# Attention and two expert layers in one kernel: first value sums and second query sums on GpSimd, the token list zeroed from a ready tile, the last gate logits ahead of the first expert job, and gate logits with the token tile as weights

## The chip, the cores and the metric

The kernel runs on one core of one Trainium2 chip. The time is device microseconds (us) for one execution. Three runs of the kernel before gave a median of 747.64 us (745.11 to 751.28). The engines are called by the names of the profile: PE is TensorE, DVE is VectorE, ACT is ScalarE, POOL is GpSimd, SP is SyncE, which issues most DMAs.

## What is computed

Attention over 4 batches, 8 heads, 576 tokens and a head width of 64, in two parts that are added; then two mixture-of-experts layers on the 2304 tokens of width 512. Each has 8 experts with a hidden width of 1024 and sends a token to one expert.

```python
q_d, k_d, v_d = (mean over groups of 4 tokens of q, k, v)
out_up    = repeat(softmax(q_d k_d^T * scale) v_d, 4)
out_local = softmax(q k^T * scale, only |i - j| < 4) v
x = out_up + out_local                       # 2304 x 512

logits = x @ w_gate;  e = argmax(logits);  g = softmax(logits)[e]
layer 1: out = g * sigmoid(x @ w_output_gate)[e] * (relu(x @ w1[e]) @ w2[e])
layer 2: the same on the result, without the sigmoid
```

## The kernel before

**Attention.** The tokens are cut into 20 tiles of 2 x 58 tokens (5 tiles a batch). For each batch the sums of 4 neighbours are formed of k (`sums_k`, L442), q (`sums_q`, L459) and v (`sums_v`, L478). From them come "pooled" scores, a softmax, and `od`, which is spread over the tiles by a matmul with `rep`. Each tile adds its local attention (class `Local`, L593). `sums_v` adds, for each of three blocks, two halves of `vraw` (L480, 128x520) and then twice 64x260 into `vpd` (L483): 3 and 6 instructions a batch. On POOL, `sums_k` and `sums_q` take two steps through a tile `tm` (L451 and L457; L475 and L476); on DVE, `sums_q` is one reduction (L473).

**The order of the work.** A prologue is written out by the string `PRO` (L72): `F` first sums, `V0` the value sums of batch 0 on DVE, `s`, `m`, `f` the pooled attention of its four head pairs, `A0` and `A2` the sums of batch 1 (the engines given by `S1` at L71: of the four letters, k and q of each half, "p" is POOL and "d" DVE), `V1` the value sums of batch 1 on POOL, `list` the opening of the token list. Then steps -1 to 22 follow, each by the string `ORDER` (L73): the pooled work of the next batch, the scores of tile s, the values of tile s-1, the transposes and logits of tile s-2, and routing. A scheduler orders the instructions of each engine from that; each engine then runs its list strictly in order and waits on semaphores.

**The token list.** `list_open` (L239) starts an accumulation of zeros in PSUM: it makes a zero tile by multiplying a constant with 0 and three copies on DVE, and one matmul (L247). Each tile then adds its tokens with one matmul (`put`, L357), made from `am`, `oc` and `bm` (L344 to L353).

**Gate logits of a tile** (L696 to L712): four matmuls with the gate columns (32) as weights and the token tile as the moving side (L377 in `logits`), a copy to SBUF on ACT (L702), and one matmul with the copied 128x128 block as weights and a selection of 16 columns (L709); then a copy on DVE (L712) into `lgs`. `route` (L251) picks the expert of each token, counts with `tri` and `ones` (L286 to L293, result `pos`), computes the place in the list (`place`, L307) and spreads it.

**Experts.** The first job (256 tokens of the largest expert, chosen by `snap` after 14 tiles) gathers its rows by indirect DMA on POOL (`fetch`, L1161; `gather`, L1149), transposes them (`xpose`, L1192; PE L1201, ACT L1205 for `xh`, DVE L1208 for `xl`) and runs `hide` (L1397): per 128 hidden units 12 matmuls (L1283 to L1285) with the weights split into `wh` and `wl` (L1122 on ACT, L1130 on DVE), then the second layer into `py`. The raw weights come through three buffers (`raw`). The second job needs the list of all 20 tiles. Behind the first job stands a loop over overflow slots (L1291), at which all engines meet; behind it come the other jobs of both layers, which fill the time from 206 us to the end.

Of the kernel before, what the change touches and what calls it, by code (L numbers as in the profile page):

```python
# [9 lines left out]
F32 = mybir.dt.float32  # L10
# [4 lines left out]
ALU = mybir.AluOpType  # L15
# [17 lines left out]
LK = E * NS  # L33
# [26 lines left out]
LGX = 1  # L60
# [7 lines left out]
QPE = 2  # L68
KPOOL = 0
Q1POOL = 0  # L70
S1 = "pdpd"  # L71
PRO = "F0 s0 V0 s1 F2 s2 s3 zq m1 Ls m0 m2 f0 f1 lqk lvr f2 m3 V1 A0 lcs rep A2 f3 Le lvw zp lw1 list"  # L72
ORDER = "R As Ae q0f Cf Xt Cp p0s Xl Xs An p0e q1f p1s q0p Cx D p1e K q1p S"  # L73

C_ID = 0
# [105 lines left out]
def moe_pair_kernel(  # L181
# [17 lines left out]
    nc = tc.nc  # L199
# [5 lines left out]
    ps_misc = ctx.enter_context(tc.tile_pool(name="ps_misc", bufs=1, space=PSUM))  # L205
# [10 lines left out]
    wgs = [const.tile([128, 4, 32], F32, name=f"wg{i}") for i in range(2)]  # L216
# [4 lines left out]
    ikey = cs[:, C_IKEY:C_IKEY + LK]  # L221
    sel = cs[:, C_SEL:C_SEL + 16]
# [12 lines left out]

    list_ps = {}
    placed = {}

    def list_open(m):  # L239
        t = ps_list.tile([128, 512], F32, tag="list", name=f"list{m}")  # L240
        z = ab.tile([128, 3 * LK], F32R, tag="bm", name="zb")
        za = ab.tile([128, 128], F32R, tag="am", name="za")
        nc.vector.tensor_scalar(z[:, 0:LK], ikey, 0.0, None, op0=ALU.mult)
        nc.vector.tensor_copy(z[:, LK:2 * LK], z[:, 0:LK].bitcast(F32))
        nc.vector.tensor_copy(z[:, 2 * LK:3 * LK], z[:, 0:LK].bitcast(F32))
        nc.vector.tensor_copy(za, z[:, 0:128].bitcast(F32))
        nc.tensor.matmul(t[:, 0:3 * LK], lhsT=za, rhs=z, start=True, stop=False, skip_group_check=True)  # L247
        nc.vector.memset(base[m], 0.0)
        list_ps[m] = t
# [125 lines left out]
    def logits(m, xT, n, lT, after=None):  # L375
        for g in range(4):
            i = nc.tensor.matmul(  # L377
                lT[32 * g:32 * g + 32, 0:n], lhsT=wgs[m][:, g, :], rhs=xT[:, g, 0:n],
                tile_position=(0, 32 * g), start=True, stop=True, skip_group_check=True,
            )  # L380
            if after is not None:
                tc.add_manual_dep(
                    i.ins, after.ins.name,
                    mybir.DependencyInfo(mybir.DependencyClass.Sync, mybir.DependencyReason.DATA),
                    reason="the four column tiles run side by side",
                )


    def attention(actx, early, early_x, front):
# [3 lines left out]
        sb2 = actx.enter_context(tc.tile_pool(name="a_sb2", bufs=2, side="right"))  # L393
# [11 lines left out]
        rep = sb1.tile([128, NTP + NP, 128], F32R, name="rep")  # L405
# [3 lines left out]
        zx = sbe.tile([128, DM], F32, name="zx")  # L409
# [68 lines left out]
        def sums_v(b, eng=nc.gpsimd):  # L478
            for k in range(3):
                eng.tensor_tensor(vraw[:, k, 0:2], vraw[:, k, 0:2], vraw[:, k, 2:4], op=ALU.add)  # L480
                for s in range(2):
                    o = slice(64 * s, 64 * s + 64)
                    eng.tensor_tensor(vpd[b % 2][o, k, s], vraw[o, k, 0], vraw[o, k, 1], op=ALU.add)  # L483
# [109 lines left out]
        class Local:  # L593
# [100 lines left out]
                front[0] = nc.scalar.copy(self.xT, self.pt)  # L694

            def lmm(self):  # L696
                self.lT = ps_misc.tile([128, 4, 128], F32, tag="misc", name="lT")
                logits(0, self.xT, 128, self.lT[:, 0])

            def ltevac(self):  # L700
                self.lts = sb2.tile([128, 128], F32, tag="lts", name="lts")
                nc.scalar.copy(self.lts, self.lT[:, 0])  # L702

            def lsel(self):
                if LGX:
                    self.lg = self.lT[:, 1, 0:16]
                else:
                    self.lg = ps_misc.tile([128, 512], F32, tag="misc", name="lg")[:, 0:16]
                nc.tensor.matmul(self.lg, lhsT=self.lts, rhs=sel, skip_group_check=True)  # L709

            def lgevac(self, lgs, j):
                nc.vector.tensor_copy(lgs[:, j], self.lg)  # L712
# [4 lines left out]
        for b in range(B):  # L717
            s0 = NTP * (b - 1) + 2
# [19 lines left out]
        wu = ps_misc.tile([128, 512], F32, tag="misc", name="wu")  # L738
        for _ in range(NWARM):
            nc.tensor.matmul(wu, lhsT=zx[:, 0:128], rhs=zx)  # L740
        load_k(0, 0, 2)
        load_q(0, 0, 2)
        nc.sync.dma_start(ident, cst[:, C_ID:C_ID + 128])
# [39 lines left out]
        def sums1(c):  # L783
            sums_k(1, c, 2, None if S1[c] == "d" else nc.gpsimd)
            sums_q(1, c, 2, None if S1[c + 1] == "d" else nc.gpsimd)

        pro = {
            "F0": lambda: first(0),
            "F2": lambda: first(2),
            "V0": lambda: sums_v(0, nc.vector),  # L790
            "Ls": lambda: (loc[0].scores(), loc[0].smax()),
            "Le": loc[0].exps,
            "rep": staged,
            "list": lambda: list_open(0),
            "zp": lambda: zero(1, nc.gpsimd, "p"),
            "zq": lambda: zero(1, nc.gpsimd, "q"),
            "lvw": lambda: load_vw(0),
# [8 lines left out]
        for c in range(NP):  # L806
            pro.update({
                f"s{c}": lambda c=c: start(c), f"m{c}": lambda c=c: middle(c), f"f{c}": lambda c=c: finish(c),
            })
        for o in PRO.split():  # L810
            pro[o]()

        for s in range(-1, NL + 3):
# [4 lines left out]
            A, C, X = get(s), get(s - 1), get(s - 2)  # L818
# [61 lines left out]
                    ]  # L880

            def xsel():
                X.lsel()
                if g[1] == 0:
                    lgst[g[0]] = sb2.tile([128, 5, 16], F32, tag="lgs", name="lgs")
                X.lgevac(lgst[g[0]], g[1])
# [11 lines left out]
                "Cx": C and C.xevac,  # L898
                "Ct": C and (lambda: (C.xflip(), C.xtevac())),
                "Xt": X and (lambda: (X.xflip(), X.xtevac())),  # L900
                "Xl": X and (lambda: (X.lmm(), X.ltevac())),
                "Xs": X and xsel,
                "K": group, "D": defer1, "R": ready1, "S": puts1,
            }
# [60 lines left out]
    def experts():  # L965
# [226 lines left out]
        def xpose(job, k):  # L1192
            if k == 0:
                xp = pl[f"x{job.i % 2}"]
                job.xT = tuple(xp.tile([128, 4, 512], F32R, tag=t, name=t) for t in ("xh", "xl"))
            xh, xl = job.xT
            mm = job.slots[k][1]
            xr = job.x[k]
            pt = psx.tile([128, 4, 128], F32, tag="m", name="t")
            for d in range(4):  # L1200
                nc.tensor.transpose(  # L1201
                    pt[:, d, 0:mm], xr[0:mm, 128 * d:128 * d + 128], ident[0:mm, 0:mm]
                )
            o = slice(128 * k, 128 * k + mm)
            i = nc.scalar.copy(xh[:, :, o], pt[:, :, 0:mm])  # L1205
            if job.i == 0:
                after.append(i)
            nc.vector.tensor_tensor(xl[:, :, o], pt[:, :, 0:mm], xh[:, :, o].bitcast(F32), op=ALU.subtract)  # L1208
# [414 lines left out]
```

## Time and profile before

| | |
|---|---|
| median of 3 runs | 747.64 us (745.11 to 751.28) |
| the profiled execution | 745.73 us |
| its span, first to last instruction | 744.0 us |
| busy in the span: PE, DVE, ACT, POOL | 94%, 61%, 46%, 23% |
| mean granted clock of PE | 0.969 of 2.4 GHz |

A row of the timeline gives the start, the busy time of what is merged in it, the engine, the line and operation, the tiles and how many records; in brackets is the idle time of the engine just before, and what ended it. On PE one matmul in full precision leaves two records. A row of stages gives the length, then the busy time and the records of each engine, the granted clock as a share of 2.4 GHz, the share of the 16 DMA engines and their rate. The order of the instructions of each engine is known for both kernels; how long they take or wait is known of the kernel before alone.

### The profile page before, as it was taken

The page shows a single profiled execution, that of the slowest core. Times are in us where ns is not written, and L with a number is a line of the kernel's source. Part 1 is how long each engine was busy: PE and PEld are TensorE (multiplying, and loading weights), DVE is VectorE, ACT ScalarE, POOL GpSimd, SP SyncE. Part 2 cuts the span into 40 slices and gives each one's busy share as a digit, 9 for nine tenths or more (in the row PEclk, how much of TensorE's full clock was granted, in tenths as well). Part 3 has the DMA queues.
Part 4 walks back from the last instruction along what each step waited for, and adds up shares of the span by engine and source line. Part 5 has one row for each costly group of instructions (what it writes and reads, how often), then busy time and mean ns, then how long its engine had stood idle before and what let it go on. Part 6 is the DMA issues. An engine that isn't in the chain of part 4 may idle for free. (4 is left out here: it accounts for less than half of the span.)

```text
span 744.0 us, 15847 instructions
## 1 busy us (share of the span) xinstructions
PE 700.1 (94%) x6048; PEld 640.2 (86%) x6048; DVE 450.5 (61%) x1173; ACT 343.5 (46%) x634; POOL 173.2 (23%) x214
## 2 busy tenths in 40 slices
PE   8699899968899999999999999989999999999993
PEld 4477677758799999999999999888999999999992
DVE  7777979758666656575766876545444454555520
ACT  4155756475245353545355464245335353554530
POOL 5285530010141202121130130142013030311211
PEclk9699999997999999999999999989999999999997
DMA  9936562143175435445554461357335454555500
GB/s 359 414 111 231 195 221 100 54 157 126 59 262 191 157 124 179 148 155 185 169 182 154 155 216 58 120 182 226 116 122 163 143 179 135 187 186 183 163 21 16
DMA packets 52990, 120.99 MB, mean 163 GB/s; under 512 B 4800, under 2 KB 26176, under 8 KB 51884
## 3 DMA queue, kind: packets, MB, share of 16 engines
q1 hardware_dynamic: 45772, 99.19, 40.0%
q0 software_dynamic: 7136, 20.72, 8.0%
q8 instruction: 50, 0.82, 0.5%
q14 instruction: 32, 0.26, 0.1%
HBM read 101.01 MB, written 20.71 MB: 164 GB/s over the span
## 5 line engine op out<-in xcount | busy, mean ns | idle before, releaser
L1122 ACT CAST wh<-raw 128x1024 fp32r<-128x1024 f32 x128 | 133.2, 1048 | 198.8 <-PE py L1284 114.3
L1130 DVE TENSOR_TENSOR wl<-raw,wh 128x1024 fp32r<-128x1024 f32 x128 | 156.2, 1224 | 111.8 <-ACT wh L1122 111.7
L1284 PE MATMUL ph<-xl,wh 128*128 128x256 f32 (+8 forms) x576 | 177.8, 310 | 0.2 <-DVE xl L1208 0.2
L1283 PE MATMUL ph<-xh,wh 128*128 128x256 f32 (+8 forms) x576 | 174.9, 312 | 2.6 <-DVE xl L1208 1.9
L1285 PE MATMUL ph<-xh,wl 128*128 128x256 f32 (+8 forms) x576 | 176.9, 308 | 0.0
L1283 PE MATMUL py<-h,wh 128*128 128x256 f32 (+8 forms) x448 | 138.6, 316 | 0.0
L1284 PE MATMUL py<-h,wh 128*128 128x256 f32 (+8 forms) x448 | 137.9, 311 | 0.0
L1285 PE MATMUL py<-h,wl 128*128 128x256 f32 (+8 forms) x448 | 137.4, 310 | 0.0
L1283 PEld LDWEIGHTS ph<-xh,wh 128*128 128x128 f32 x576 | 110.4, 195 | 5.1 <-DVE xl L1208 2.0
L1284 PEld LDWEIGHTS ph<-xl,wh 128*128 128x128 f32 x576 | 111.1, 193 | 1.1 <-DVE xl L1208 0.5
L1285 PEld LDWEIGHTS ph<-xh,wl 128*128 128x128 f32 x576 | 111.2, 193 | 0.6
L1410 DVE SCALAR_TENSOR_TENSOR h<-ph,h 128x256 fp32r<-128x256 f32 (+8 forms) x144 | 66.3, 471 | 41.7 <-ACT h L1409 41.2
L1409 ACT ACTIVATE h<-ph 128x256 fp32r<-128x256 f32 (+8 forms) x144 | 60.5, 422 | 55.8 <-PE ph L1285 54.6
L1284 PEld LDWEIGHTS py<-h,wh 128*128 128x128 f32 x448 | 84.3, 189 | 0.6
L1285 PEld LDWEIGHTS py<-h,wl 128*128 128x128 f32 x448 | 84.2, 188 | 0.6
L1283 PEld LDWEIGHTS py<-h,wh 128*128 128x128 f32 x448 | 83.6, 188 | 0.8
L1151 POOL DMA_INDIRECT xr<-x,ri x49 | 52.1, 1063 | 98.1 <-PE t L1201 77.2
L1211 POOL DMA_INDIRECT out<-yr,ri x25 | 25.8, 1031 | 127.4 <-ACT yr L1229 83.0
L1211 POOL DMA_INDIRECT x<-yr,ri x24 | 24.7, 1027 | 127.1 <-ACT yr L1229 119.9
L1201 PE MATMUL t<-ident,xr 128*128 128x128 f32 (+5 forms) x196 | 30.2, 275 | 8.7 <-DMA xr<-x,ri 8.7
L1208 DVE TENSOR_TENSOR xl<-t,xh 128x512 fp32r<-128x512 f32 (+5 forms) x49 | 30.1, 620 | 13.2 <-ACT xh L1205 13.0
L1205 ACT CAST xh<-t 128x512 fp32r<-128x512 f32 (+5 forms) x49 | 26.1, 532 | 24.4 <-PE t L1201 21.2
(194 smaller groups left out, 1012.1 us busy)
## 6 DMA issues: line engine op xcount, KB each, us to landing
raw<-w_a SPq DMA_DIRECT2D x64, 512.0 KB
raw<-w_b SPq DMA_DIRECT2D x64, 512.0 KB
vraw<-vr SPq DMA_DIRECT2D x4, 1560.0 KB
vd<-vw SPq DMA_DIRECT2D x4, 1280.0 KB
kd<-kT SPq DMA_DIRECT2D x8, 586.0 KB
qt<-qT SPq DMA_DIRECT2D x8, 586.0 KB
x<-zx SPq DMA_DIRECT2D x6, 768.0 KB
x<-x SPq DMA_DIRECT2D x36, 116.0 KB
```

The source lines that it names most:

```text
L1122: i = nc.scalar.copy(hi, raw)
L1130: i = nc.vector.tensor_tensor(lo, raw, hi.bitcast(F32), op=ALU.subtract)
L1151: g = nc.gpsimd.indirect_dma_start(xr[0:mm], None, src, bass.IndirectOffsetOnAxis(ap=ri[0:mm, k, 0:1], axis=0))
L1201: nc.tensor.transpose(pt[:, d, 0:mm], xr[0:mm, 128 * d:128 * d + 128], ident[0:mm, 0:mm])
L1205: i = nc.scalar.copy(xh[:, :, o], pt[:, :, 0:mm])
L1208: nc.vector.tensor_tensor(xl[:, :, o], pt[:, :, 0:mm], xh[:, :, o].bitcast(F32), op=ALU.subtract)
L1211: i = nc.gpsimd.indirect_dma_start(M.dst[:, :], bass.IndirectOffsetOnAxis(ap=ri[0:mm, k, 1:2], axis=0), yr[0:mm], None, bounds_check=NT - ...
L1283: nc.tensor.matmul(ps, lhsT=ah, rhs=bh, start=first, stop=False)
L1284: nc.tensor.matmul(ps, lhsT=ah, rhs=bl, start=False, stop=False)
L1285: nc.tensor.matmul(ps, lhsT=al, rhs=bh, start=False, stop=last)
L1409: nc.scalar.activation(a[:, 0:n], ph[:, 0:n], func=AF.Relu)
L1410: nc.vector.scalar_tensor_tensor(b_[:, 0:n], ph[:, 0:n], 0.0, a[:, 0:n].bitcast(F32), op0=ALU.max, op1=ALU.subtract)
```

## The change

Four edits. The value sums of batch 0 and both query sums of batch 1 go to POOL (`V0`, and `S1` from "pdpd" to "pppp"). The list of layer 1 is opened at the very start from the zero tile `zx`, with two copies in place of four instructions. The four logits matmuls of a tile take the token tile as weights and 16 gate columns as the moving side, add up in PSUM, and give the logits without the copy on ACT and the selecting matmul. And the transposes of the first job may stand on PE only behind the last tile's logits.

```diff
-S1 = "pdpd"
-PRO = "F0 s0 V0 s1 ... f3 Le lvw zp lw1 list"
+S1 = "pppp"
+PRO = "F0 s0 V0 s1 ... f3 Le lvw zp lw1"
...
-    def list_open(m):
+    def list_open(m, zeros=None):
...
+        if zeros is not None:
+            nc.vector.tensor_copy(z, zeros[:, 0:3 * LK])
+            nc.vector.tensor_copy(za, zeros[:, 0:128])
...
             def lmm(self):
-                self.lT = ps_misc.tile([128, 4, 128], F32, tag="misc", name="lT")
-                logits(0, self.xT, 128, self.lT[:, 0])
-
-            def ltevac(self):
-                self.lts = sb2.tile([128, 128], F32, tag="lts", name="lts")
-                nc.scalar.copy(self.lts, self.lT[:, 0])
-
-            def lsel(self):
...
-                nc.tensor.matmul(self.lg, lhsT=self.lts, rhs=sel, skip_group_check=True)
+                self.lg = ps_misc.tile([128, 512], F32, tag="misc", name="lg")[:, 0:16]
+                for d in range(4):
+                    last[0] = nc.tensor.matmul(
+                        self.lg, lhsT=self.xT[:, d], rhs=wgs[0][:, d, 0:16], start=(d == 0), stop=(d == 3)
+                    )
...
+        list_open(0, zx)
         load_k(0, 0, 2)
...
-            "V0": lambda: sums_v(0, nc.vector),
+            "V0": lambda: sums_v(0),
...
             for d in range(4):
-                nc.tensor.transpose(
+                i = nc.tensor.transpose(
...
+                if job.i == 0:
+                    tc.add_manual_dep(
+                        i.ins, last[0].ins.name,
...
+                        reason="the last tokens' logits go ahead",
+                    )
```

Below, three places where the order of an engine moves. Names with a number are one buffer each; lines from 240 on stand a few lines higher or lower in the changed kernel (L480 becomes L485, L483 becomes L488, L1201 becomes L1197, L1283 to L1285 become L1285 to L1287).

On POOL, the prologue before: the zeroing of both `vpd` buffers is followed by the key sums of batch 1 (kd_100).

```order
L412 MEMSET vpd_110 32x3x260
L412 MEMSET vpd_111 64x3x260
L412 MEMSET vpd_111 32x3x260
L412 MEMSET vpd_111 64x3x260
L412 MEMSET vpd_111 32x3x260
L451 ISA
L451 TENSOR_TENSOR tm<-kd_100 128x576
L457 TENSOR_TENSOR kpd_108<-tm 64x288 x2
```

On POOL, the same place now, where L485 and L488 are the value sums of batch 0.

```order
L417 MEMSET vpd_110 32x3x260
L485 ISA
L485 TENSOR_TENSOR vraw<-vraw 128x520 x3
L488 TENSOR_TENSOR vpd_110<-vraw 64x260 x4
L456 TENSOR_TENSOR tm<-kd_100 128x576
L488 TENSOR_TENSOR vpd_110<-vraw 64x260 x2
L417 MEMSET vpd_111 64x3x260
L417 MEMSET vpd_111 32x3x260
```

Nine value sums now stand ahead of all sums of batches 1 and 2, and half of the zeroing has moved behind them.

On PE, the end of the counting before, which stands between the two groups of the first job's transposes (L1201); L377 and L709 are the last tile's logits, L1283 and L1284 the first matmuls of `hide` (x on the right is a count).

```order
L293 MATMUL pos<-ohb,cb 128x8
L1201 MATMUL t<-ident,xr 128x128 x4
L377 MATMUL lT<-xT,wg_79 32x128 x4
L1283 MATMUL ph<-xh,wh 128x256 x4
L709 MATMUL lT<-cs,lts 128x16
L1283 MATMUL ph<-xh,wh 128x256
L1284 MATMUL ph<-xl,wh 128x256
```

On PE, the end of the same counting now (L704 are the new logits, L1197 the first job's transposes, L1285 the first matmuls of `hide`, L362 two additions to the list):

```order
L298 MATMUL pos<-ohb,cb 128x8
L704 MATMUL lg<-wg_79,xT 128x16 x4
L1197 MATMUL t<-ident,xr 128x128 x8
L1285 MATMUL ph<-xh,wh 128x256 x5
L362 MATMUL list_123<-bm,am 128x432 x2
L1286 MATMUL ph<-xl,wh 128x256
```

The counting and the last logits have moved ahead of the first job's transposes, and two additions to the list stand earlier in `hide`.

On PE, the prologue before: L559 are the pooled value products, of which the first nine need `vpd`, L545 the transposes of the fourth head pair.

```order
L545 MATMUL t<-ident,pd_114 128x128 x3
L559 MATMUL v<-vpd_110,pts 128x130 x9
L247 MATMUL list_319<-zb,za 128x432
L545 MATMUL t<-ident,pd_115 128x128 x3
L559 MATMUL v<-vpd_110,pts 128x130 x3
```

The same place on PE now:

```order
L550 MATMUL t<-ident,pd_114 128x128 x3
L564 MATMUL v<-vpd_110,pts 128x130 x9
L550 MATMUL t<-ident,pd_115 128x128 x3
L564 MATMUL v<-vpd_110,pts 128x130 x3
```

The matmul that opens the list is gone from between the value products. Behind the branch at the overflow loop the instructions of every engine stand in the same order in both kernels.

## Rows read from the trace of the kernel before

**Rows 1.** Stages: length, busy time (records) of PE, PEld, DVE, ACT, POOL, clock, DMA.

```profile
0.00:23.00 23.00, 16.50 (x108) 10.11 (x108) 17.37 (x29) 7.62 (x15) 13.71 (x24) 0.96 0.94 370
23.00:37.00 14.00, 10.33 (x45) 7.02 (x45) 8.94 (x26) 2.36 (x5) 1.40 (x2) 0.57 1.02 420
37.00:54.20 17.20, 16.29 (x297) 11.98 (x297) 13.14 (x28) 9.29 (x20) 16.17 (x18) 1.00 0.26 87
54.20:160.00 105.80, 99.70 (x1752) 80.40 (x1750) 86.35 (x296) 65.81 (x160) 27.07 (x29) 1.00 0.47 165
...
168.00:178.00 10.00, 7.87 (x46) 6.63 (x45) 9.13 (x33) 3.52 (x5) 0.00 (x0) 0.50 0.58 196
...
206.00:744.00 538.00, 523.60 (x3604) 499.93 (x3600) 295.42 (x679) 239.60 (x394) 109.69 (x131) 0.98 0.48 155
```

**Rows 2.** Who waited for whom, PE, 0 to 45 us: total, times, longest.

```profile
PE v L559 <- DVE vpd L483: 3.8, 3, 2.3
PE list L247 <- DVE za L246: 3.0, 1, 3.0
```

**Rows 3.** Timeline of DVE, 13 to 24 us: start, busy time, instruction.

```profile
14.18 1.91 DVE L480 TENSOR_TENSOR vraw<-vraw 128x520 f32<-128x520 f32 x3
...
19.48 3.36 DVE L483 TENSOR_TENSOR vpd<-vraw 64x260 f32<-64x260 f32 x4
```

**Rows 4.** Timeline of POOL, 0 to 55 us.

```profile
2.27 6.26 POOL L412 MEMSET vpd<- 64x780 f32 x8
...
48.97 5.07 POOL L483 TENSOR_TENSOR vpd<-vraw 64x260 f32<-64x260 f32 x6
```

**Rows 5.** POOL by line and form, 0 to 100 us: count, busy us, mean ns.

```profile
L483 POOL TENSOR_TENSOR vpd<-vraw 64x260 f32<-64x260 f32 x18 | 14.6, 812 | 1.1
L480 POOL TENSOR_TENSOR vraw<-vraw 128x520 f32<-128x520 f32 x9 | 12.0, 1363 | 12.3 <-DMA vraw<-vr 12.3
...
L475 POOL TENSOR_TENSOR tm<-qt 128x576 f32<-128x576 f32 x4 | 5.3, 1331 | 0.4 <-DMA qt<-qT 0.2
...
L476 POOL TENSOR_TENSOR qd<-tm 128x288 f32<-128x288 f32 x4 | 2.7, 667 | 0.2
```

**Rows 6.** Timeline of PE at two points of the prologue.

```profile
36.97 0.39 PE L654 MATMUL v<-odh,rep 128*128 128x256 f32 x1
...
54.16 1.50 PE L559 MATMUL v<-vpd,pts 128*128 128x130 f32 x12
```

**Rows 7.** Timeline of PE, one tile's logits, each with the row behind it.

```profile
45.37 0.43 PE L377 MATMUL lT<-xT,wg 128*32 128x128 f32 x8
45.73 0.75 PE L510 MATMUL s<-kpd,qd 128*128 128x288 f32 x2
...
47.37 0.29 PE L709 MATMUL lT<-cs,lts 128*128 128x16 f32 x2
47.51 0.52 PE L545 MATMUL t<-ident,pd 128*128 128x128 f32 x3
```

**Rows 8.** Timeline of all engines, 167 to 206 us, at the first job.

```profile
167.25 1.09 PE L1201 MATMUL t<-ident,xr 128*128 128x128 f32 x4 [5.23 <-DMA xr<-x,ri]
...
168.57 0.19 DVE L309 TENSOR_TENSOR pe<-pos,base 128x32 f32<-128x32 f32 x1 [6.01 <-PE pos L293]
...
169.52 0.58 ACT L1205 CAST xh<-t 128x512 fp32r<-128x512 f32 x1 [0.51 <-PE t L1201]
...
172.76 0.68 DVE L1208 TENSOR_TENSOR xl<-t,xh 128x512 fp32r<-128x512 f32 x1
...
173.50 0.58 PE L1283 MATMUL ph<-xh,wh 128*128 128x256 f32 x1 [1.88 <-DVE xl L1208]
...
174.25 0.58 PE L1284 MATMUL ph<-xl,wh 128*128 128x256 f32 x1 [0.16 <-DVE xl L1208]
...
178.98 1.33 ACT L348 ACTIVATE bm<-oc,v 128x144 fp32r<-128x144 f32 x4
...
205.45 0.93 PE L377 MATMUL lT<-yT,wg 128*32 128x256 f32 x8 [2.48 <-DVEq L1291]
```

More of the change, by code (lines that the diff above doesn't have):

```diff
@@ L70 @@
 Q1POOL = 0
-S1 = "pdpd"
-PRO = "F0 s0 V0 s1 F2 s2 s3 zq m1 Ls m0 m2 f0 f1 lqk lvr f2 m3 V1 A0 lcs rep A2 f3 Le lvw zp lw1 list"
+S1 = "pppp"
+PRO = "F0 s0 V0 s1 F2 s2 s3 zq m1 Ls m0 m2 f0 f1 lqk lvr f2 m3 V1 A0 lcs rep A2 f3 Le lvw zp lw1"
 ORDER = "R As Ae q0f Cf Xt Cp p0s Xl Xs An p0e q1f p1s q0p Cx D p1e K q1p S"
@@ L237, in moe_pair_kernel @@
     placed = {}
-    def list_open(m):
+    last = [None]
+    def list_open(m, zeros=None):
         t = ps_list.tile([128, 512], F32, tag="list", name=f"list{m}")
@@ L242, in list_open @@
         za = ab.tile([128, 128], F32R, tag="am", name="za")
[L243 to L246, printed above, removed]
+        if zeros is not None:
+            nc.vector.tensor_copy(z, zeros[:, 0:3 * LK])
+            nc.vector.tensor_copy(za, zeros[:, 0:128])
+        else:
+            nc.vector.tensor_scalar(z[:, 0:LK], ikey, 0.0, None, op0=ALU.mult)
+            nc.vector.tensor_copy(z[:, LK:2 * LK], z[:, 0:LK].bitcast(F32))
+            nc.vector.tensor_copy(z[:, 2 * LK:3 * LK], z[:, 0:LK].bitcast(F32))
+            nc.vector.tensor_copy(za, z[:, 0:128].bitcast(F32))
         nc.tensor.matmul(t[:, 0:3 * LK], lhsT=za, rhs=z, start=True, stop=False, skip_group_check=True)
@@ L696, in lmm @@
             def lmm(self):
-                self.lT = ps_misc.tile([128, 4, 128], F32, tag="misc", name="lT")
-                logits(0, self.xT, 128, self.lT[:, 0])
-            def ltevac(self):
-                self.lts = sb2.tile([128, 128], F32, tag="lts", name="lts")
-                nc.scalar.copy(self.lts, self.lT[:, 0])
-            def lsel(self):
[L705 to L708, printed above, removed]
-                nc.tensor.matmul(self.lg, lhsT=self.lts, rhs=sel, skip_group_check=True)
+                self.lg = ps_misc.tile([128, 512], F32, tag="misc", name="lg")[:, 0:16]
[3 more added lines that the diff above has]
+                    )
             def lgevac(self, lgs, j):
@@ L793, in attention @@
             "rep": staged,
-            "list": lambda: list_open(0),
             "zp": lambda: zero(1, nc.gpsimd, "p"),
@@ L882, in xsel @@
             def xsel():
-                X.lsel()
                 if g[1] == 0:
@@ L900, in attention @@
                 "Xt": X and (lambda: (X.xflip(), X.xtevac())),
-                "Xl": X and (lambda: (X.lmm(), X.ltevac())),
+                "Xl": X and X.lmm,
                 "Xs": X and xsel,
@@ L1200, in xpose @@
             for d in range(4):
-                nc.tensor.transpose(
+                i = nc.tensor.transpose(
                     pt[:, d, 0:mm], xr[0:mm, 128 * d:128 * d + 128], ident[0:mm, 0:mm]
                 )
+                if job.i == 0:
+                    tc.add_manual_dep(
+                        i.ins, last[0].ins.name,
+                        mybir.DependencyInfo(mybir.DependencyClass.NoSync, mybir.DependencyReason.DATA),
+                        reason="the last tokens' logits go ahead",
+                    )
             o = slice(128 * k, 128 * k + mm)
```

## The prediction

> **What bounds the kernel now.** I read the stages first. From 206 us to the end PE is busy 523.6 of 538 us [rows 1], and from the branch at the overflow loop, which PE leaves at 205.45 [rows 8], every engine runs the same instructions in the same order in both kernels. All queues are empty at that branch. So the question is only how much earlier the branch comes.
>
> Ahead of it lie four stretches. From 54.2 to 160 us PE is busy 99.7 of 105.8 us [rows 1]: PE sets the pace of the steady part of attention. From 23 to 37 us PE runs at 0.57 of its clock and DVE is busy 8.9 of 14 us [rows 1]; the waits of PE show why it had nothing to do: 3.8 us for the value sums on DVE and 3.0 us for the zeros that open the list [rows 2]. From 37 to 54.2 us the row to look at is POOL's: 16.17 of 17.2 us [rows 1]. It ends with the value sums of batch 1, from 48.97 to 54.04 [rows 4], and at 54.16 PE starts the products that read them [rows 6]. POOL is thus at the end of its tether there, although the chain of waits names it nowhere. The last stretch is the start of the first expert job. PE waits 5.23 us for the gathered rows, until 167.25; DVE waits 6.01 us for a count that stands on PE behind these transposes; and when the rows are there, PE waits once more, 1.88 us, for `xl`, since DVE first has to make up what it missed [rows 8]. From 168 to 178 us the granted clock is 0.50, the lower level, 1.2 GHz [rows 1].
>
> **The change, part by part.** The sum is made against the profiled execution, 745.73 us for a span of 744.0; the median of the three runs lies 1.9 above it.
>
> *Value and query sums to POOL.* DVE loses the three adds from 14.18 and the six that end at 22.84 [rows 3], two query reductions, and four instructions for the zeros. For PE the prologue becomes shorter: the zeros are there at the start, and behind the value products come only the fourth head pair and the last pooled scores. The value sums now end on POOL: they can start by 14.2 (DVE started them then without waiting for the load [rows 3]) and take 3 x 1.36 + 6 x 0.81 = 9.0 us [rows 5], with one key sum of some 1.1 between them: 24.3, against 22.84 on DVE. From there PE has some 2.4 us of products, the fourth pair with 2.9, and 3.4 of scores at the low clock (my estimates from how the same work ran from 22.9 to 36.97): 33, less about 1 if the clock rises earlier, so `L654` starts near 32 in place of 36.97 [rows 6], 5 us earlier.
>
> But POOL now has a list without a gap. Up to 54.04 it was busy 13.71 + 1.40 + 16.17 = 31.3 us [rows 1]. Of that about 5.1 lie ahead of 14.2: its first 2 us and half of the eight `vpd` zeroings, 6.26 / 2 = 3.1 [rows 4]; the other half has moved behind the value sums. So 31.3 - 5.1 = 26.2 us of old work remain, plus 9.0 of value sums, plus query sums of 2 x 1.33 + 2 x 0.67 = 4.0 [rows 5]: 39.2, and the value sums of batch 1 end at 14.2 + 39.2 = 53.4 instead of 54.04. PE comes to these products near 50 and waits. In that wait it has already done the scores of the next tile, some 1.2 us that stood behind the products. So of 5 us about 0.6 + 1.2 = 1.8 are left; I take 2.0. The bounds: 5 us if POOL isn't late at all; nothing, if its adds go a tenth slower than their means or the load lands 2 us later.
>
> *The list opened at the start.* Two copies on DVE and a matmul in a time when the first keys are still being loaded: nothing, and the 3.0 us wait is in the 5 above.
>
> *New logits, 20 tiles.* Before, the four matmuls of a tile hold PE for 45.73 - 45.37 = 0.36 us and the selecting one for 47.51 - 47.37 = 0.14 [rows 7]: 0.50. Now there are four of the selecting one's shape (128 weight columns, 16 moving): 4 x 0.14 = 0.56. That is +0.06 x 20 = 1.2 us on the engine that sets the pace. Against it stand 20 copies less on ACT and shorter waits of PE in the steady part, which are 6 us in all over its 105.8 [rows 1]. I put both together at 0, between -3 and +4.
>
> The low end of 0.14 is what a rule speaks against. The Trainium skill ("TensorE: Matmul & The Clock Gate", LDWEIGHTS) says that the load of weights takes a time that goes with their columns, not their rows. By its formula, an estimate, a tile's loads would grow from some 0.43 to 0.85 us, and the sum below by 8.5 us if none of them were hidden. The trace agrees with the direction of it, but the 0.14 between two starts shows most of a load lying beside other work; so the sum goes by 0.14.
>
> *The last list entries of the first job.* On PE the additions to the list that the first gather needs stand a little earlier among the last tiles' work. That is worth up to 2 us, but the gather also shares the DMA engines with the last rows' stores, and DVE must have split three weight blocks by then. I take 0.5, between 0 and 2.
>
> *Last logits and count ahead of the transposes.* Count from the landing of the gathered rows, 167.25 [rows 8]. Before, PE is at its first low-part matmul at 174.25, 7.0 us later. Now the count and the logits run while PE would wait; DVE does the places and the three weight splits, the 4.2 us from 168.57 to 172.76, in its old wait of 6.01 [rows 8]. What is late next: two transposes of 1.09 each (+2.2), the second `xh`, 0.58 (+2.8), then four `bm` on ACT, 1.33 (+4.1) [rows 8], for two additions to the list that now stand ahead of the low parts; the second takes some 0.7 at this clock, estimated from the 0.58 of a 256-column matmul. So +4.9 in place of +7.0: 2.1 gained. `xl`, twice 0.68, is ready by +3.6 and not late. Then the clock: between 174.25 and 178 the old kernel works at half speed, 3.75 us for 1.9 us' worth. If the higher level comes back earlier, because PE isn't interrupted for 1.88 us, up to 1.9 are saved; I take 1.2. Together 3.3, between 1 and 6 (2.1 + 1.9, and 2 more if the wait is too short for the clock to fall). The second job's list is made from the last tile's logits, which come over 10 us earlier, so its gather should move with PE.
>
> Sum: 2.0 + 0 + 0.5 + 3.3 = 5.8 us, 745.7 - 5.8 = 739.9 by the profiled execution, and 747.6 - 5.8 = **741.8** by the median.
>
> **The rivals.**
> - *POOL eats the prologue and no more than that.* The value sums of batch 1 arrive when they did, PE waits for all of its gain, 5 us. For it: 16.17 of 17.2 us [rows 1]. Against: POOL stood idle for most of 23 to 37 us (busy 1.40 [rows 1]), and that is what the added work fills. Without the 2.0: 743.8.
> - *Everything works.* POOL isn't late (5), the gather comes 1 us earlier, the clock never falls for long (6): 12 us, 735.6. Against it: the list of POOL above.
> - *The weight loads show.* Each of the new logits' matmuls holds PE for its whole recorded 0.29 us [rows 7], not 0.14: 4 x 0.29 - 0.50 = 0.66 per tile, 13.2 in all, 755.0, slower than before. It decides from 5.8 / 20 = 0.29 per tile on, that is 0.2 us per matmul. For it: four loads of 128 columns in a row, with little matmul beside each. Against: transposes of that size run back to back elsewhere without it. The rule on weight loads named above belongs here.
> - *The branch doesn't move with the first job.* It waits for the second job's rows, and if DVE is the bound between, busy 9.13 of 10 us from 168 to 178 [rows 1], the 3.3 are lost: 745.1.
>
> **How the numbers follow.** The forecast gets 0.61, with a range of its own from 737 to 746; POOL 0.12; everything works 0.13; the weight loads 0.06; the branch 0.08. A measurement of this kernel can tell about 1% from no change, 7.5 us: faster by more means below 740.2, slower means above 755.1. Faster: all of "everything works" and 0.25 of the forecast's 0.61, 0.38. Slower: half of the weight loads and a little for a worse order, 0.05. The rest, 0.57, is the same. The range from 734 to 749 leaves out the weight loads and the ends of the others.
>
> **What would show it.** In the new profile the value products of batch 0 should wait for POOL until about 24, `L659` (before L654) should start near 32, and PE should wait for POOL's L488 for 2 to 4 us between 49 and 54, the sums there ending between 52 and 55. ACT has 20 copies less; PE's steady part keeps its length of 105 us within 3. At the first job DVE's long wait for the count should be gone, and the low parts should start 4 to 6 us after the rows land; the branch should come near 199.5. The forecast is wrong if POOL ends those sums before 51 or after 57, if four new logits hold PE for more than 0.8 us, or if PE or DVE waits between the first job's landing and the branch as long as before.

## The result and the profile after

The changed kernel takes 753.01 us (median of 9 runs, 750.09 to 755.27), the kernel before 746.86 (9 runs). The ratio is 1.0075, with a 95% interval from 1.005 to 1.0101: slower by three quarters of a percent, where 741.8 was forecast and 749.0 was the end of the range. The profiled execution is 754.75 us with a span of 753.0.

The stages first, cut where the same work ends now (columns as in [rows 1]):

```profile
23.00:37.00 14.00, 11.61 (x67) 7.17 (x71) 4.24 (x12) 1.73 (x4) 13.27 (x18) 0.59 1.01 422
37.00:54.20 17.20, 16.51 (x315) 13.15 (x307) 13.61 (x30) 8.73 (x18) 16.55 (x19) 1.00 0.35 123
54.20:172.00 117.80, 106.48 (x1674) 89.37 (x1673) 92.92 (x299) 61.80 (x144) 28.90 (x32) 0.97 0.43 143
176.00:186.00 10.00, 8.12 (x40) 6.88 (x41) 6.27 (x18) 3.96 (x9) 0.00 (x0) 0.66 0.56 197
214.00:753.00 539.00, 524.24 (x3608) 500.56 (x3608) 295.26 (x679) 240.09 (x394) 107.41 (x133) 0.98 0.47 154
```

Behind the branch nothing changed: 753.0 - 214.04 = 539.0 us now, 744.0 - 205.45 = 538.6 before (in the profiled executions of the experiments below it is 535.9 to 540.1). The whole loss lies ahead of it, and there in the steady part of attention: it ran to 160 and now runs to 172.

PE at the points that the prediction named:

```profile
24.18 2.53 PE L564 MATMUL v<-vpd,pts 128*128 128x130 f32 x10 [1.81 <-POOL vpd L488]
...
35.39 0.38 PE L659 MATMUL v<-odh,rep 128*128 128x256 f32 x1
...
53.53 0.71 PE L564 MATMUL v<-vpd,pts 128*128 128x130 f32 x4
56.06 0.52 PE L550 MATMUL t<-ident,pd 128*128 128x128 f32 x3 [1.82 <-DVE pd L536]
...
176.09 0.66 PE L1197 MATMUL t<-ident,xr 128*128 128x128 f32 x4
177.46 0.89 PE L1197 MATMUL t<-ident,xr 128*128 128x128 f32 x4 [0.71 <-DMA xr<-x,ri]
...
181.88 0.46 PE L1286 MATMUL ph<-xl,wh 128*128 128x256 f32 x1
...
214.04 0.64 PE L382 MATMUL lT<-yT,wg 128*32 128x256 f32 x8 [2.36 <-DVEq L1293]
```

The prologue is 1.6 us shorter (35.39 against 36.97, [rows 6]); the rows of the first job land 8.8 us later (176.09 against 167.25, [rows 8]) and the branch comes 8.6 us later.

Where the time goes in between is read best from one work that every tile has: the transposes of its `x` (L690 before, L695 now). The table gives their start in the profiled execution of before, and for the other kernels how much later (+) or earlier (-) they start; the branch stands behind. It is used for all experiments below.

Two things help to read it. Ahead of each of these points every kernel has the same work on PE (but for the logits), except at tile 3: there the kernels with both query sums on POOL (`S1 = "pppp"`) have already done 16 products with the repeated rows (L667), 1.7 us, that stand behind it in the others. Tile 4 is therefore the fair point for the prologue. And the changed kernel and `u_dep` have the same instructions in the same order on PE, DVE, ACT and POOL up to tile 20; the 2.7 us by which they differ at tile 1, and the up to 2.0 us behind it, are what two single executions differ by.

| kernel | tile 1 | 3 | 4 | 6 | 7 | 8 | 9 | 20 | branch |
|---|---|---|---|---|---|---|---|---|---|
| before, at us | 42.92 | 57.90 | 66.18 | 73.32 | 80.96 | 90.96 | 101.72 | 161.23 | 205.45 |
| changed | -1.6 | +2.0 | +1.3 | +2.7 | +5.7 | +11.1 | +8.9 | +12.0 | +8.6 |
| u_logits: old logits, rest changed | -2.2 | +0.8 | -0.3 | 0.0 | -0.7 | +4.1 | +2.2 | +1.3 | +2.3 |
| a_logits: new logits alone | +0.3 | +1.0 | +2.4 | +3.3 | +6.8 | +12.4 | +10.2 | +14.5 | +11.5 |
| u_pool: all sums as before | +0.2 | +1.0 | +2.4 | +3.3 | +6.8 | +13.1 | +10.9 | +14.7 | +10.0 |
| u_dep: without the rule | -4.3 | +2.4 | +1.7 | +2.6 | +4.9 | +12.1 | +9.8 | +14.0 | +11.2 |
| u_S1: query sums on DVE | -2.2 | -1.5 | -0.1 | +0.8 | +4.3 | +10.0 | +7.8 | +11.5 | +6.3 |
| ul_nodep: POOL and list alone | -2.9 | 0.0 | -1.2 | -0.9 | -1.2 | +3.3 | +1.3 | +0.9 | +0.7 |
| ul_pin3: u_logits, casts in order | -2.9 | 0.0 | -1.2 | -0.9 | -1.2 | +3.3 | +1.3 | +0.1 | -3.1 |
| ul_S1_pin3: the same, query sums on DVE | -4.6 | -4.5 | -4.6 | -4.6 | -4.6 | -4.6 | -3.2 | -3.9 | -7.5 |
| ulp_pin3: the same, all sums as before | +0.6 | +0.6 | +0.6 | +0.6 | +0.6 | +0.6 | +2.5 | +1.5 | -2.0 |
| ul_V0_pin3: ul_pin3, value sums on DVE | -3.5 | -0.1 | -1.1 | -0.1 | -0.3 | +2.3 | +0.3 | -0.1 | -3.1 |

The gain of the prologue is gone at tile 4; between tiles 6 and 9 another 6.2 us are lost; after that it is 0.3 us a tile; and 3.4 us come back from the last tile to the branch.

PE's longest waits from 36 to 110 us, total, times and longest, in the changed kernel:

```profile
PE pos L291 <- DVE lgs L709: 3.0, 1, 3.0
PE list L362 <- ACT bm L353: 2.2, 2, 1.8
PE t L550 <- DVE pd L536: 1.8, 1, 1.8
```

None of them is among the longer waits of the kernel before, where the first count waits 0.3 us and the longest wait in this stretch is 1.9 us, for `am` from DVE.

### The profile page after: what moved, and what is told of

Same layout as the page of the kernel before. It is cut to its first block, busy times and chain, and to the rows that moved or that the text cites. A ratio compares the mean times of both kernels' runs of the same rounds, so it can differ in the third digit from the quotient of the medians.

```text
span 753.0 us, 15752 instructions
## 1 busy us (share of the span) xinstructions
PE 709.8 (94%) x6008; PEld 652.0 (87%) x6008; DVE 451.4 (60%) x1160; ACT 338.5 (45%) x614; POOL 183.6 (24%) x227
## 5 line engine op out<-in xcount | busy, mean ns | idle before, releaser
L1287 PE MATMUL ph<-xh,wl 128*128 128x256 f32 (+8 forms) x576 | 176.6, 308 | 0.0
L1285 PE MATMUL ph<-xh,wh 128*128 128x256 f32 (+8 forms) x576 | 174.6, 311 | 1.7 <-ACT xh L1207 1.4
L1285 PE MATMUL py<-h,wh 128*128 128x256 f32 (+8 forms) x448 | 138.5, 316 | 0.0
L1287 PE MATMUL py<-h,wl 128*128 128x256 f32 (+8 forms) x448 | 137.4, 310 | 0.0
L1285 PEld LDWEIGHTS ph<-xh,wh 128*128 128x128 f32 x576 | 110.3, 194 | 4.0 <-ACT xh L1207 2.2
L1287 PEld LDWEIGHTS ph<-xh,wl 128*128 128x128 f32 x576 | 111.0, 193 | 0.6
L1287 PEld LDWEIGHTS py<-h,wl 128*128 128x128 f32 x448 | 84.1, 188 | 0.6
L1285 PEld LDWEIGHTS py<-h,wh 128*128 128x128 f32 x448 | 83.4, 188 | 0.9
L1147 POOL DMA_INDIRECT xr<-x,ri x49 | 49.9, 1018 | 101.4 <-PE t L1197 77.1
L1213 POOL DMA_INDIRECT out<-yr,ri x25 | 25.8, 1030 | 128.9 <-ACT yr L1231 84.6
L1213 POOL DMA_INDIRECT x<-yr,ri x24 | 24.6, 1025 | 126.2 <-ACT yr L1231 119.3
L1485 DVE COPY yT<-py 128x256 f32<-128x256 f32 (+8 forms) x28 | 13.7, 489 | 39.6 <-PE py L1287 39.6
```

Source lines behind the costliest of these rows:

```text
L1147: g = nc.gpsimd.indirect_dma_start(xr[0:mm], None, src, bass.IndirectOffsetOnAxis(ap=ri[0:mm, k, 0:1], axis=0))
L1213: i = nc.gpsimd.indirect_dma_start(M.dst[:, :], bass.IndirectOffsetOnAxis(ap=ri[0:mm, k, 1:2], axis=0), yr[0:mm], None, bounds_check=NT - ...
L1285: nc.tensor.matmul(ps, lhsT=ah, rhs=bh, start=first, stop=False)
L1287: nc.tensor.matmul(ps, lhsT=al, rhs=bh, start=False, stop=last)
L1485: nc.vector.tensor_copy(yT[:, dc, 0:n], py[:, 0:n])
```

## The experiments

**One part undone at a time, and the logits alone.** Two theories stood against each other. L: the new logits hold PE longer than the old ones, four matmuls of 0.20 us in place of 0.14. P: the sums on POOL, which now lie elsewhere, slow DVE's routing of the first tiles.

The row for L, PE and its weight loads at one tile's logits in the changed kernel, to be read against [rows 7]:

```profile
43.70 0.96 PE L704 MATMUL lg<-wg,xT 128*128 128x16 f32 x8
44.51 0.73 PE L515 MATMUL s<-kpd,qd 128*128 128x288 f32 x2
...
43.46 1.10 PEld L704 LDWEIGHTS lg<-wg,xT 128*128 128x128 f32 x8
```

From the start of the logits to the next matmul PE is held for 44.51 - 43.70 = 0.81 us, where it was 0.50, and the weight loads fill that time from end to end.

`u_logits` puts the old three steps back:

```diff
-                self.lg = ps_misc.tile([128, 512], F32, tag="misc", name="lg")[:, 0:16]
-                for d in range(4):
-                    last[0] = nc.tensor.matmul(self.lg, lhsT=self.xT[:, d], ...)
+                logits(0, self.xT, 128, self.lT[:, 0])
...
+                last[0] = nc.tensor.matmul(self.lg, lhsT=self.lts, rhs=sel, skip_group_check=True)
```

> The changed kernel with the old gate logits (four matmuls with the gate columns as weights, copy on ACT, selecting matmul), the other three edits kept. Theory L (the new logits hold PE for 0.81 us a tile in place of 0.50, 20 x 0.31 = 6.2 us): the time falls by about 6, to 747. Theory P (the sums on POOL now lie beside the routing of the first tiles and slow DVE there; PE waits 3.0 us at the first count and 2.2 us at the first additions to the list and the clock falls): the order of POOL's sums stays as in the changed kernel, so the wait at the first count stays above 2 us and the time above 750.

Measured: 746.48 us, ratio to before 0.9993 (0.9961 to 1.0025). The 6.5 us are gone, and with them PE's wait at the first count; the longest wait is now a later one, at the list:

```profile
PE list L362 <- ACT bm L353: 3.1, 1, 3.1
```

That is theory L's number, and P as it was written is contradicted: POOL's order stayed.

`u_pool` takes the sums back to DVE:

```diff
-S1 = "pppp"
+S1 = "pdpd"
...
-            "V0": lambda: sums_v(0),
+            "V0": lambda: sums_v(0, nc.vector),
```

> The changed kernel with the value sums of batch 0 and the query sums of batch 1 back on DVE (V0 and S1 as before), the other three edits kept. Theory P: PE's wait at the first count falls below 1 us, the last tile's transposes come some 8 us earlier, the time falls to about 745 to 746. Theory L: nothing of the 6.2 us comes back and the 1.6 us won in the prologue are lost: 753 to 755.

Measured: 754.22 us, 1.0087 (1.0061 to 1.0113). Nothing comes back, and PE's wait at the first count is still there (3.2 us). The sums that were moved are not the cause of the loss. That POOL slows DVE at the routing is not ruled out by this: in this kernel too POOL works without a gap from 70.1 to 86.0, beside the routing.

`u_dep` leaves out the rule of the first job:

```diff
-                if job.i == 0:
-                    tc.add_manual_dep(i.ins, last[0].ins.name, ...)
```

> The changed kernel without the rule that the last tile's logits stand ahead of the first job's transposes. If that rule is what made up 3.4 us between the last tile's transposes (12.0 us late) and the branch (8.6 late), the time rises by about 3, to 756. If the logits of the last tile find their place without it, the time stays within 1 us of 753.

Measured: 756.05 us (four runs), 1.0103 (1.0056 to 1.0151). That is 3.0 more than the changed kernel by the medians and 2.1 by the ratios, and the two intervals lie over each other. In the traces the branch comes 2.6 us later than in the changed kernel, and 2.0 of that stand already at tile 20, where the two kernels have not yet differed; these are not the rule's. What the rule does is seen behind the landing of the rows, in the kernel without it:

```profile
177.01 0.63 PE L1197 MATMUL t<-ident,xr 128*128 128x128 f32 x4 [1.15 <-DMA xr<-x,ri]
...
181.49 1.86 PE L704 MATMUL lg<-wg,xT 128*128 128x16 f32 x8 [1.68 <-DVE base L316]
...
184.40 0.41 PE L1280 MATMUL ph<-xl,wh 128*128 128x256 f32 x1
```

From the rows to the first low part it takes 184.40 - 177.01 = 7.4 us here and 181.88 - 176.09 = 5.8 with the rule; to the branch it takes 39.6 and 38.0. The rule does help, by 1.6 us in these traces; that the whole 3.0 us are its work is not shown.

`a_logits` is the kernel before with the new logits and nothing else.

> The kernel before with the new gate logits alone. Theory L: PE is held 0.31 us longer at each of 20 tiles, the time rises by about 6, to 753. Theory P: the sums of batch 0 and 1 stay on DVE, so nothing new lies beside the routing: within 1.5 us of before, 746 to 748.

Measured: 755.39 us, 1.0107 (1.0072 to 1.0142): 9.1 us more than before by the medians, 8.0 by the ratio. PE waits 3.2 us at the first count here too, though the sums are where they were. The new logits bring that wait with them.

**Is it the hold on PE, or a buffer?** The counts and the logits share one PSUM buffer, so the first count waits until DVE has copied the logits of the sixth tile. That copy comes late on DVE, at 84.16 in the changed kernel (the timeline of DVE):

```profile
77.79 0.68 DVE L639 TENSOR_REDUCE sm<-p 128x8 f32<-128x512 f32 x1
...
78.59 0.62 DVE L640 TENSOR_SCALAR sm<-sm 128x8 f32<-128x8 f32 x1
...
79.57 1.41 DVE L642 TENSOR_TENSOR p<-p,sm 128x512 f32<-128x512 f32 x1
80.90 1.17 DVE L331 TENSOR_SCALAR ez<-ez 128x5 f32<-128x5 f32 x1
...
84.16 0.16 DVE L709 COPY lgs<-lg 128x16 f32<-128x16 f32 x1
```

Theory S says that this buffer is the loss. `actlg` lets ACT make the copy:

```diff
-                nc.vector.tensor_copy(lgs[:, j], self.lg)
+                nc.scalar.copy(lgs[:, j], self.lg)
```

> The changed kernel with the copy of the logits out of PSUM on ACT in place of DVE. Theory S (there is one buffer for logits and counts, so PE's first count waits until the copy of the logits has come through DVE's queue; 3.0 us, and then the clock falls): PE's wait at the first count falls below 1 us, the seventh and eighth tile come 3 to 5 us earlier, 748 to 750. Theory L (only the time that the new matmuls hold PE matters): the wait moves to the next place, the additions to the list, and the time stays at 752 to 754.

Measured: 753.37 us (four runs), 1.0108 (1.0068 to 1.0147). The wait at the first count is gone, and another stands in its place:

```profile
PE t L550 <- ACT pd L543: 2.7, 1, 2.7
```

And ACT stands for DVE before it:

```profile
82.99 0.44 ACT L543 ACTIVATE pd<-pd 128x288 f32<-128x288 f32 x1 [3.40 <-DVE pd L536]
```

S falls: PE waits there for whatever comes from a late DVE, by one way or another.

`dbl` issues the four new matmuls of each tile twice, to price them by themselves:

```diff
-                for d in range(4):
+                for d in list(range(4)) * 2:
```

> The changed kernel with the four new logits matmuls of each tile issued twice (the second set overwrites the first, the logits are the same): 80 more matmuls of that shape. Theory L (each holds PE for 0.20 us, 0.81 us for four): 80 x 0.20 = 16 us more, 769. The forecast's value of 0.14: 11 us more, 764. If their weight loads lie beside other work: 753 to 757.

Measured: 772.7 us (four runs), 1.0308 (1.0257 to 1.0358): 19.7 us more than the changed kernel for 80 matmuls, 0.25 us each. One tile of it on PE:

```profile
49.82 1.85 PE L704 MATMUL lg<-wg,xT 128*128 128x16 f32 x16
51.53 0.52 PE L550 MATMUL t<-ident,pd 128*128 128x128 f32 x3
```

51.53 - 49.82 = 1.71 us for eight, 0.21 each. They hold PE for that time, hardly anything hides it, and somewhat more than it arrives at the end. The forecast's 0.14 would have given 11 us.

**What the other three edits are worth.** Without the logits they should have given 5.8 us; `u_logits` shows 0. Two things were found there. The first is at the first job. ACT in that kernel, whose lines stand a few rows lower (L1213 casts the rows to `xh`, L1124 casts a weight block):

```profile
168.92 0.58 ACT L1213 CAST xh<-t 128x512 fp32r<-128x512 f32 x1 [2.10 <-PE t L1203]
175.13 1.04 ACT L1124 CAST wh<-raw 128x1024 fp32r<-128x1024 f32 x1 [5.62 <-DMA raw<-w_a]
176.08 0.58 ACT L1213 CAST xh<-t 128x512 fp32r<-128x512 f32 x1
```

And PE, behind it:

```profile
176.71 1.44 PE L1291 MATMUL ph<-xh,wh 128*128 128x256 f32 x5 [6.23 <-ACT xh L1213]
```

The second half of the rows was ready, but in ACT's list it stood behind the fourth weight block, whose load ended at 175. `ul_nodep` takes the rule away as well; `ul_pin3` keeps it and lets that cast stand only behind both halves (in the kernel a constant, `PINX`, chooses the block that waits for the rows; the same constant chooses the block whose split on DVE stands behind the places of the last tokens, so that moves with it):

```diff
-PINX = 4
+PINX = 3
```

> The changed kernel with the old logits and without the rule on the first job's transposes: the sums on POOL and the list opened at the start alone. If what the prologue wins is lost at the sums of batch 1 and at the routing of the first tiles (2.2 us late at the ninth tile with these edits): 747 to 749. If it is kept: 743 to 745.

> The changed kernel with the old logits, and on ACT the fourth weight block's cast may stand only behind both casts of the first job's rows (in the kernel with the old logits alone the second cast stands behind it and waits with it for the weights until 175). If that order is what took the gain of the first job: the low parts start near 172 in place of 179.4, the value from the rows to the second layer falls from 24.9 to about 21 us, the time to 742 to 744. If the weights' arrival sets the pace anyway: within 1 us of 746.5.

Measured: `ul_nodep` 746.35 us, 0.9996 (0.9975 to 1.0018), just under what its first branch gave; `ul_pin3` 743.32, 0.9947 (0.9924 to 0.997). ACT in `ul_pin3`, where both halves now come ahead of the weight block:

```profile
167.67 0.59 ACT L1213 CAST xh<-t 128x512 fp32r<-128x512 f32 x1 [2.07 <-PE t L1203]
169.57 0.59 ACT L1213 CAST xh<-t 128x512 fp32r<-128x512 f32 x1 [1.31 <-PE t L1203]
173.78 1.04 ACT L1124 CAST wh<-raw 128x1024 fp32r<-128x1024 f32 x1 [3.63 <-DMA raw<-w_a]
```

And PE there, from the transposes of the rows to the first low part:

```profile
166.52 1.11 PE L1203 MATMUL t<-ident,xr 128*128 128x128 f32 x4 [0.26 <-DMA xr<-x,ri]
168.41 1.12 PE L1203 MATMUL t<-ident,xr 128*128 128x128 f32 x4 [0.78 <-DMA xr<-x,ri]
...
171.44 0.41 PE L1292 MATMUL ph<-xl,wh 128*128 128x256 f32 x1
```

From the rows to the low parts it is 4.9 us. The prediction had 4.9 too, but from other terms: two additions to the list ahead of the low parts, which stand behind them here, and no wait for the second half of the rows; that the numbers meet is luck. With the old logits the rule is worth nothing by itself and 3.0 us together with the order of the casts; what that order is worth without the rule was not tried.

The second thing is POOL. Its list in the changed kernel, from the sums of batch 2 on:

```profile
55.25 1.15 POOL L456 TENSOR_TENSOR tm<-kd 128x576 f32<-128x576 f32 x1
...
67.96 3.96 POOL L485 TENSOR_TENSOR vraw<-vraw 128x520 f32<-128x520 f32 x3 [10.01 <-DMA vraw<-vr]
...
74.44 4.74 POOL L488 TENSOR_TENSOR vpd<-vraw 64x260 f32<-64x260 f32 x6
79.26 1.17 POOL L456 TENSOR_TENSOR tm<-kd 128x576 f32<-128x576 f32 x1
```

The value sums have moved ahead of the rest of the key and query sums, wait 10 us for their load with POOL idle, and what is queued behind them runs until 84, beside the routing. Before, these sums were done in that gap, and POOL was free at 82.75. Theory Q: this order costs what the prologue wins. `ul_S1_pin3` is `ul_pin3` with `S1 = "pdpd"`, `ulp_pin3` has `V0` on DVE as well, and `ul_V0_pin3` has `V0` on DVE and `S1 = "pppp"`.

> As the kernel with the old logits and the fixed order of the casts, but the query sums of batch 1 back on DVE (S1 as before); the value sums of batch 0 stay on POOL. With them POOL's later order is the one of before again: one half's key and query sums of batch 2 stand ahead of the value sums that wait 10 us for their load. Theory Q (that order pushes 5 us of sums beside DVE's routing of the first tiles and costs 2 to 2.5 us at the eighth tile): the ninth tile's transposes come 2 us earlier than in the kernel compared, the time falls to 741. Rival (the order on POOL is worth nothing): 743 to 744.

> The list opened at the start, the rule on the first job's transposes and the fixed order of the casts alone; all sums as before, old logits. If the sums on POOL are worth nothing in sum, 743 to 744, as with them. If they win 2 us in the prologue that stay: 745 to 746. If they cost 1 to 2 us (theory Q): 741 to 742.

> As the kernel with the old logits and the fixed order of the casts, but the value sums of batch 0 back on DVE; the query sums of batch 1 stay on POOL. POOL's order after that is a third one. If only the prologue counts: the first product of the attention with the repeated rows comes 1 to 2 us later than with both on POOL and the time is 744 to 745. If the loss at the sums of batch 1 goes with it: 743.

Measured: 740.98 us, 0.993 (0.9897 to 0.9962); 743.07, 0.9929 (0.9901 to 0.9957); 742.6, 0.994 (0.9915 to 0.9965). POOL in `ul_S1_pin3`:

```profile
45.17 5.09 POOL L488 TENSOR_TENSOR vpd<-vraw 64x260 f32<-64x260 f32 x6
...
59.66 1.15 POOL L456 TENSOR_TENSOR tm<-kd 128x576 f32<-128x576 f32 x1 [1.84 <-DMA kd<-kT]
65.57 3.96 POOL L485 TENSOR_TENSOR vraw<-vraw 128x520 f32<-128x520 f32 x3 [4.77 <-DMA vraw<-vr]
...
77.53 0.67 POOL L481 TENSOR_TENSOR qd<-tm 128x288 f32<-128x288 f32 x1
```

And in `ul_pin3` the value sums of batch 1:

```profile
49.63 4.74 POOL L488 TENSOR_TENSOR vpd<-vraw 64x260 f32<-64x260 f32 x6
```

With the early order the 4.6 us won in the prologue are still there, whole, at the eighth tile (table), and 3.2 at the ninth; `ul_pin3` is 2.9 ahead at the first and 1.3 behind at the ninth. But little of that is the order that Q names. Of the 4.5 us between the two kernels at tile 9, 1.7 are there at tile 1; 1.7 more come up to tile 4, where the value sums of batch 1 end on POOL at 54.37 in `ul_pin3` and at 50.26 here, since the query sums no longer stand ahead of them; only 1.1 come between tiles 4 and 9, where the order for batch 2 matters. Each of these parts is no larger than what two executions of the same instructions differ by, and the edit changes both things at once. The times don't settle it either: the three intervals lie over each other, so what the sums on POOL are worth in the end, between 0 and 2 us, is not settled by these runs, and Q is not shown. The third kernel keeps its time with a prologue gain of 3.5 us of which 1.1 are left at tile 4.

`u_S1` asks the same of the changed kernel, with the new logits:

> The changed kernel with only the query sums of batch 1 back on DVE; the value sums of batch 0 on POOL, the new logits, the list and the rule kept. If moving the query sums is what lost the prologue's gain: at the third tile's transposes it is still 2 to 4 us ahead of before (the changed kernel: 2.0 behind), and the time falls by 2 to 3, to 750 to 751. If the new logits lose it in any case, since with them POOL's order for batch 2 is the late one here too: 752 to 754.

Measured: 753.7 us, 1.0077 (1.0049 to 1.0105). At the third tile it is 1.5 us ahead of before, short of the 2 of the first branch, and at tile 4 by 0.1; from tile 6 to tile 9 it loses 7.0 us, and the time is the second branch's. With the new logits POOL gets the late order in any case, so no kernel here has the new logits and the early order.

`ul_S1_pin3`, at 740.98 us, has the lowest median of all and is faster than both kernels: the new prologue for the value sums, the list opened at once, the rule and the order of the casts, without the new logits and with the query sums on DVE. By its ratio it is not ahead of `ulp_pin3`, which has all sums as before.

## Why the prediction was wrong

**The step that failed** is "New logits, 20 tiles. ... I put both together at 0, between -3 and +4." It cost 753.01 - 746.48 = 6.5 us with the other edits there, and 9.1 alone, outside its bounds. I had taken 0.14 us a matmul from the selecting one of [rows 7]. That is one matmul between larger ones, and its two weight loads lay beside the one ahead. Four in a row, each with 128 weight columns and 16 moving, have nothing long enough to hide the next load; they go at the pace of the loads, 0.20 us each. Added up over the 20 tiles and without waits, the logits held PE for 12.6 us before and hold it for 18.2 now: 5.6 more, 0.28 a tile, next to the 0.29 from which the rival "the weight loads show" was to decide. The sign that the prediction itself gave, more than 0.8 us for four, came with 0.81. What I put against the rival speaks for it: the transposes of `x`, with one load each, start 0.11 us apart at the full clock, and so do the two records that each new matmul leaves. The rival got 0.06; its 755.0 is the nearest number in the text, in part by luck, for it came from 0.66 a tile, over twice the hold that was measured. The rule of the Trainium skill ("TensorE: Matmul & The Clock Gate", LDWEIGHTS) that I had weighed against the row was right: its estimate of 0.85 us a tile stands beside the measured 0.81.

From tile 6 to tile 9 there is more than hold: 6.2 us in the changed kernel and 6.9 in `a_logits`, where three tiles of hold are 0.9. This stretch before, in the changed kernel and in `u_logits` (columns as in [rows 1]):

```profile
73.32:101.72 28.40, 25.82 (x394) 20.29 (x391) 24.32 (x81) 17.73 (x46) 17.99 (x20) 1.00 0.49 171
76.02:110.62 34.60, 28.78 (x384) 23.79 (x383) 28.95 (x81) 16.94 (x42) 16.23 (x18) 0.90 0.50 167
73.31:103.92 30.61, 27.21 (x393) 21.45 (x392) 25.37 (x81) 17.47 (x45) 19.23 (x22) 0.94 0.47 163
```

Of the 6.2 us, 3.2 are time in which PE does nothing (34.60 - 28.78 = 5.8 us in place of 2.6), mostly waiting for a late DVE; 0.9 are the hold; and some 2 are left, with the granted clock at 0.90 in place of 1.00. And DVE is not late by its order alone: the same number of its instructions, 81, takes 28.95 us in place of 24.32. In `u_logits`, with the same late list on POOL and the old logits, it takes 25.37 and the stretch 2.2 us more than before, so that list alone does not do it. Why DVE's instructions take so much longer with the new logits was not tried; the last section shows some that meet POOL's. Some of the loss comes back later, in the wait for the first rows.

**"2.0 of the prologue are left"**: the first half was right. The value products waited for POOL until 24.18 (forecast: about 24), and `L659` came at 35.39 here, and at 32.4 to 35.4 in the traces with these sums on POOL (forecast: 32). The batch 1 sums ended at 49.63 + 5.54 = 55.17, forecast 53.4. The wait of 2 to 4 us for them that was forecast is not there; PE begins their products at 53.53 and then waits 1.82 us for `pd` from DVE. I had looked at POOL's list only up to these sums, and the query sums on POOL moved the order behind them too. With the old logits and both sums on POOL, 0.3 to 1.2 us of the gain are left at tile 4 and none at tile 9. The rival "POOL eats the prologue" had the loss right.

**"The list opened at the start: nothing"** and **the last list entries, 0.5**: nothing contradicts the first, and no run shows the second by itself. Of the 12.0 us by which the last tile was late, the rows were only 8.8 late; 3.2 fell into PE's old wait for them, 5.23 us in [rows 8], which in the changed kernel is one of 0.71.

**The first job, 3.3**: this was too high as well. By the prediction's own count, from the landing of the rows, the low parts came after 5.8 us in place of 7.0 (forecast: 4.9), for the second half of the rows landed later (the wait of 0.71) and PE stood for `xh` and `xl` once more. At the branch hardly anything is left of it, 38.0 us behind the rows in place of 38.2: ACT had to wait for the next weight block (last section). In `u_pool` and `u_S1`, which have the rule and the new logits too, it is 36.2 and 35.5, so the size of this term, between 0 and 3 us, is not settled. The hope for the clock did not hold: it was at 0.50 from 178 to 184 in the changed kernel as well. In the kernel with the old logits the gain turned into a new wait, behind a weight block that was not there yet; that case was not among the rivals.

Put together from single edits by the medians: +9.1 for the new logits alone, -3.0 for the rule, about nothing for the sums and the list give +6.1; measured is 753.01 - 746.86 = +6.2, where the sum said -5.8. By the ratios it is +8.0 - 2.1 = +5.9 against +5.6. Each of these has an interval of some 2 to 4 us to either side, so that they meet so closely is luck.

## What to carry to other kernels

In these kernels a matmul with few moving columns cost what its weights cost to load (0.20 us, two loads), unless a longer matmul ran beside that load (0.14): read the weight-load rows and the distance from start to start in a run of the same kind, not at a single one between larger neighbours. When work is moved to an engine that serves its list in order, look through that list well past the moved work, for an instruction that now waits for a transfer with ready work behind it; one cast behind one late weight block took the gain of a right idea here. And undo the parts one by one: the whole change was slower, while three of its four ideas, put in the right order, were faster than the kernel before. Before a difference between two traces is given to an edit, look at what two kernels differ by where they are still the same.

## What the runs showed that I had not expected

A small instruction on DVE that met one of POOL's large ones ended with it. In the rows above a `TENSOR_SCALAR` on 128x5 takes 1.17 us, until 82.07, and one on 128x8 takes 0.62, until 79.21; the latter instruction with POOL idle, at another tile of the changed kernel:

```profile
58.43 0.17 DVE L640 TENSOR_SCALAR sm<-sm 128x8 f32<-128x8 f32 x1
```

POOL at the time of the former, until 82.04:

```profile
80.39 1.65 POOL L480 TENSOR_TENSOR tm<-qt 128x576 f32<-128x576 f32 x1
```

The reduction at 77.79, beside POOL's value sums (74.44 to 79.18), kept its 0.68. The Trainium skill ("SBUF — State Buffer", Who interferes with whom) says that DVE and GpSimd share a pair of ports that one holds for a whole instruction, and that reductions don't contend; these rows agree.

A load of one weight block took 3.4 us from issue to use before (170.46 to 173.86) and 8.9 in the changed kernel. The issues on SP, before and in the changed kernel, with the next two close behind the first in both:

```profile
170.46 2.75 SPq L1083 DMA_DIRECT2D raw<-w_a  x3
...
176.78 3.56 SPq L1079 DMA_DIRECT2D raw<-w_a  x3
```

And ACT, which waits for the first of them, before and in the changed kernel:

```profile
173.86 1.04 ACT L1122 CAST wh<-raw 128x1024 fp32r<-128x1024 f32 x1 [3.40 <-DMA raw<-w_a]
...
185.72 1.05 ACT L1118 CAST wh<-raw 128x1024 fp32r<-128x1024 f32 x1 [5.53 <-DMA raw<-w_a]
```

Why it was so much longer was not tried.

The prologue differs from run to run by when the clock comes back. The same thirteen matmuls (L524) took 4.34 us in the changed kernel and 2.46 in `u_dep`, whose instructions are the same up to there and whose granted clock from 23 to 30 us was 0.65, not 0.50. A microsecond or two at the first tile in the table is therefore no effect of an edit, and a change of that size from tile to tile shows nothing by itself either.
